# Three moves in a written-out order: the last low part of wo, the counting of tile 0, and the values' sums of the first pair

## The chip, the cores and the metric

The kernel runs on one core of a Trainium2 chip. The metric is the device time of one execution in microseconds; three runs of the kernel before took 380.36, 379.77 and 380.67, the median 380.36. Five engines work side by side, each in its own order: TensorE (PE, with its weight loads PEld), VectorE (DVE), ScalarE (ACT), GpSimd (POOL), and SyncE (SP), which issues transfers. An instruction that needs another engine's result waits for it, and everything behind it on its own engine waits too.

## The reference

x has 2048 rows of 512. Two branches are computed from it and mixed by a gate, `g*a + (1-g)*b` with `g = sigmoid(x . gate_w)`.

- Branch a is linear attention with 32 heads of 16: `q, k, v = x @ wqkv`; q and k go through a small matrix per head and two softmaxes over 16 (of the value and of its negative), which gives 32 features per head; `kv = phi_k^T v`, `z = sum phi_k`, `o = phi_q kv / (phi_q z)`, and `a = o @ wo`.
- Branch b is a choice of one of 256 experts per head: 32 heads, two scores over 16 keys each, the best key of each half; the pair names one of 256 rows of u and v; `b = sum over heads of gelu(x . u_e) * v_e`. The softmax is over one element, so it is 1. What is left is a count: how often each of the 256 experts was chosen by the 32 heads of a row, times gelu(x . u_e), times v.

## The kernel before

The rows are cut into 16 tiles of 128. Numbers are kept as a high and a low part (names ending in h and l): ScalarE casts the high part, VectorE or GpSimd subtracts it from the raw number, and three matmuls replace one. The order of every engine is the order in which the code is written (`manual_schedule`), so moving a line moves instructions on its engine.

**First half, up to about 125 us: keys, values and expert scores.** Tiles 0 to 4 are done one by one, tiles 5 to 14 in pairs (t, t+1) with t = 5, 7, 9, 11, 13. A pair shares matmuls by sums of its two tiles (class `Sums`). In a pair the banks a (pk), b (pu), c (pv), d (pk of the second tile) and e (pe) are built up with copies between them: `act.copy(b, a)` at line 487, `act.copy(c, b)` at 511, `act.copy(d, b)` at 543. The values of the second tile, vn, begin as a copy of e (line 554 in the first pair), and two sums follow on VectorE, vt = c + vn (557) and vn = b + vn (558). `k_exp` and `k_sum` (267, 271, 272) are the exponentials and sums of the key features. `Sums.high` (183) and `Sums.low` (189) make the high part gh and the low part gl of a tile's sum. The bank pu of the pair t = 7 is filled at line 487 once the pair before has read its bank by line 557.

**Second half: one turn of a loop for each tile a = 0 to 14**, with three tiles in flight: a (query projection, softmax differences and exponentials), b = a - 1 (comparison results counted, the query features transposed) and z = a - 2 (numerator, output). TensorE's order in a turn: `mid_num(z)` (matmuls oT from the transposed features pt and kvb, line 776), `front_q(a)` (pq, 56 to 58), `back(z)` (po: twelve matmuls at 888 with o's parts and wo's, then six at 895 with the coefficients ch and cl and the expert rows), `mid_mask(a)` (mk, 795), `front_s(a+1)` (the two halves of the scores s), `front_p(a+1)` (pp). The others feed it:

- `join(b)` (767), ScalarE: pt from two transposes tp; `mid_num` reads it in two halves.
- `count` (803 to 835), VectorE: a chain of 18 instructions, cut into steps by `yield`, that turns the mask into the counts cf. `step(b, n)` runs n steps, `drain(b)` the rest. Line 811 and 813 are one step. In turn 0 the first five steps of tile 0 have run; in turn 1 the rest runs.
- `coef` (839), GpSimd: cf times gelu (`gelu_out`, 662, is just ahead of it). `c_planes` (844, 846): ScalarE's copy plc and SyncE's transpose tpc. `c_join` (851, 855): ctj and the high part ch. `back_cl` (876): the low part cl on VectorE.
- `best(a+1, half)` (733, 734), VectorE: the maximum over 16 scores and the comparison with it; `turn_eq` (740) transposes the result (et).
- `soft_sum` (694), `soft_y` (704), VectorE: sums of tile a's exponentials and of the weighted w, which GpSimd makes at 690.
- `gelu_act` (656 to 658), ScalarE: the end of gelu for tile a.

The raw wo comes in late: two of its four pieces lie in rawo2, in the pool `late`. The last piece's high part is cast at line 984, its low part wol[3] is made at line 1041 (tile wbl, whose room it reuses). In turn 1 the pool `late` is closed and a new pool w4 is opened in its room; pt, plc, tpc, ctj, ch and cl lie in w4. The first join writes pt there, so it has to wait for the last reader of what lay there.

Of the kernel before, what the change touches and what calls it, by code (L numbers as in the profile page):

```python
# [16 lines left out]
ALU = mybir.AluOpType  # L17
# [18 lines left out]
def mix_kernel(ctx, tc, xT, wqT, wkT, wv, wphi, wo, wq, kk, ug, ev, cst, out):  # L36
    nc = tc.nc
    pe, dve, act, pool, sp = nc.tensor, nc.vector, nc.scalar, nc.gpsimd, nc.sync
# [210 lines left out]
    by16 = lambda a: a.rearrange("p (h f) -> p h f", f=F)  # L249
# [19 lines left out]
    def k_sum(t):  # L269
        d, st = phis[t], stk[t]  # L270
        dve.tensor_reduce(st[:, 64:128], g64(d), axis=AX.X, op=ALU.add)  # L271
        dve.reciprocal(st[:, 128:192], st[:, 64:128])
# [22 lines left out]
    def score_planes(j):  # L295
        pl = wa_.tile([P, 2, D], U16, tag="wpl", bufs=1, name=f"wpl{j}")
        act.copy(pl, wsP.pop(j).bitcast(U16).rearrange("p (c j) -> p j c", j=2))
        tp = wa_.tile([P, 8, P], U16, tag="wtp", bufs=1, name=f"wtp{j}")
        sp.dma_start_transpose(tp, pl.rearrange("p j c -> p (j c)"))
        joins.append((j, tp))  # L300
# [168 lines left out]
    for t in range(5, NT - 1, 2):  # L469
        n = t + 1  # L470
        more = [u for u in (t + 4, t + 5) if u < NT]
        for u in more:
            x_load(u)
        if t == NT - 5:
            rawu = [spare(ug[:, 0:2], "rawu0", [P, 2, NU])]
        elif t == NT - 3:
            rawu.append(spare(ug[:, 2:4], "rawu1", [P, 2, NU]))
            rawe = [spare(ev[:, 0], "rawe0", [P, D])]
        if behind:
            k_diffs(behind)  # L480
        for u in (t + 2, t + 3):
            if u < NT - 1 and u not in (7, 9):
                x_low(u)
        a = pks[t] = mm_bank(f"pk{t}")
        prod(a, tile_of(t, 0), b11, True)
        b = mm_bank(f"pu{t}")
        act.copy(b, a)
        if 5 < t < NT - 3:
            Sums.add(t + 2)
        if t == 5:  # L490
            (j1, tp), = joins
            joins.clear()
            tj1 = wa_.tile([P, D], F32, tag="wtj", bufs=1, name="wtj1")
            join_tp(j1, tp, tj1)
            score_planes(2)
            load_wq()
            load_wq()
            join_end(j1, tj1)
            Sums.add(t + 2)
        elif t < NT - 3:  # L500
            join_all()
        else:
            (j6, tp), = joins
            joins.clear()
            tj6 = wa_.tile([P, D], F32, tag="wtj", bufs=1, name="wtj6")
            join_tp(j6, tp, tj6)
        e = tr_bank(f"pe{t}")
        prod(e, sums(0, 2), b1, True)
        prod(b, sums(1, 0), b2, False)
        c = mm_bank(f"pv{t}")  # L510
        act.copy(c, b)
        if t == 5:
            k_exp(4)
            k_sum(4)
            k_mult(4)
            x_high(9)
            (j2, tp), = joins
            joins.clear()
            tj2 = wa_.tile([P, D], F32, tag="wtj", bufs=1, name="wtj2")
            join_tp(j2, tp, tj2)  # L520
        prod(a, tile_of(t, 2), b21, False)
        k_diffs(t)
        if behind:
            k_exp(behind)
            k_sum(behind)
            k_mult(behind)
        score(2, 5 < t < NT - 3)
        if t == NT - 3:
            rawq = stage(wqT, "rawq")
            score_planes(7)  # L530
        elif t > 5:
            load_wq()
            load_wq()
        for u in (t - 3, t - 2):
            kvacc(u)
        vn, vt = v_tile(n), v_tile(t)
        if t > 5:
            act.copy(vn, by16(e))
            k_exp(t)
            k_sum(t)  # L540
        prod(b, sums(0, 0), b3, False)
        d = pks[n] = mm_bank(f"pk{n}")
        act.copy(d, b)
        if t == 5:
            join_high(j2, tj2)
            score_planes(3)
            Sums.high(7, (0,))
            k_exp(t)
            x_low(9)
            k_sum(t)  # L550
        prod(c, sums(1, 2), b22, False)
        if t == 5:
            Sums.high(7, (1,))
            act.copy(vn, by16(e))
        if t == NT - 3:
            x_split(NT - 1)
        dve.tensor_tensor(vt, by16(c), vn, op=ALU.add)
        dve.tensor_tensor(vn, by16(b), vn, op=ALU.add)
        o2 = d.rearrange("p (c n) -> p c n", c=2)
        prod(o2, tile_of(n, 2), b4, False)  # L560
        if t + 3 < NT:
            if t > 5:
                Sums.high(t + 2)
            Sums.low(t + 2)
            if t == 5:
                join_low(j2, tj2)
        if t == 7:
            for i in range(2):
                x_parts(i, 11)
        for u in more if n < NT - 4 else ():  # L570
            if u != 9:
                x_high(u)
        k_mult(t)
        behind = n
    t = NT - 1
# [36 lines left out]
    def step(t, n=1):  # L612
        for _ in range(n):
            if t in chains and next(chains[t], None) is None:
                del chains[t]
# [221 lines left out]
    def coef(t):  # L837
        e = st8[t]
        (pool if t < NT - 2 else dve).tensor_tensor(e["C"], e["C"], e["G"], op=ALU.mult)

    def c_planes(t):
        e = st8[t]
        pl = w4.tile([P, 2, NX], U16, tag="plc", bufs=1, name=f"plc{t}")
        act.copy(pl, e["C"].bitcast(U16).rearrange("p (c j) -> p j c", j=2))
        e["tc"] = w4.tile([P, 4, P], U16, tag="tpc", bufs=1, name=f"tpc{t}")
        sp.dma_start_transpose(e["tc"], pl.rearrange("p j c -> p (j c)"))
# [124 lines left out]
    for a in range(NT - 1):  # L971
        n, b, z = a + 1, a - 1, a - 2
        owed = min(18, 3 * max(0, a - DEFER))
        left = min(18, 3 * max(0, a - DEFER + 1))
        B, Z = b >= 0, z >= 0
        if Z:
            mid_num(z)
        if a == 2:
            c_planes(z)
            gelu_pre(a)  # L980
        if a == 1:
            front_q(a)
            v15 = vproj(NT - 1)
            act.copy(woh[3], rawo[3])
        if B:
            planes(b, 0)
            if Z:
                c_join(z)
            if a == 1:
                v15()  # L990
            planes(b, 1)
        if a > 1:
            front_q(a)
        if owed:
            back(z - 1, owed)
            store(z - 1)
        gelu_in(a)
        if Z:
            num_lo(z)
        if B:  # L1000
            if a == 1:
                for _ in gate(a):
                    pass
                soft_in(a)
                step(b, 6)
            else:
                soft_in(a, dealt(a, b, z))
                drain(b)
        else:
            for _ in gate(a):  # L1010
                pass
        if a != 1:
            gelu_act(a)
        if a > 0:
            soft_exp(a)
        if Z and not left:
            back(z)
            store(z)
        if not left and a > 1:
            mid_mask(a)  # L1020
        if a:
            front_s(n, 0)
        if left or a == 1:
            mid_mask(a)
            if 0 < left < 18:
                back(z, 18 - left)
        if a == 1:
            kvacc(NT - 1)
            kv_final()
            cl_.close()  # L1030
            w4 = ctx.enter_context(tc_pool("w4", "right"))
        front_s(n, 1)
        front_p(n, False)
        soft_w(a)
        if a == 1:
            best(n, 0)
        soft_sum(a, 0)
        soft_sum(a, 1)
        if a == 1:
            drain(b)  # L1040
            dve.tensor_tensor(wol[3], rawo[3], woh[3], op=ALU.subtract)
        if a == 0:
            pool.tensor_tensor(wol[2], rawo[2], woh[2], op=ALU.subtract)
            step(a, 5)
        if a != 1:
            best(n, 0)
        if a == 0:
            best(n, 1)
            turn_eq(n)
        soft_y(a, 0)  # L1050
        soft_y(a, 1)
        soft_p(a)
        if B:
            join(b)
            gelu_out(b)
            coef(b)
            if a == 1:
                gelu_act(a)
            else:
                c_planes(b)  # L1060
        if a == 0:
            soft_b(a, lambda t: None)
        else:
            soft_b(a)
            best(n, 1)
            turn_eq(n)
        if a != 1:
            gelu_pre(n)
# [123 lines left out]
```

## Time and profile before

| | us |
|---|---|
| median of three runs | 380.36 (379.77 to 380.67) |
| profiled execution, its own time | 380.58 |
| its span, first to last instruction | 378.8 |
| TensorE busy | 367.2 (97%) |
| VectorE busy | 333.3 (88%) |
| ScalarE busy | 256.5 (68%) |
| GpSimd busy | 204.9 (54%) |

A line of the timeline gives start, duration, engine, line of the kernel, operation, output and inputs, shape, how many instructions were merged, and in brackets how long the engine stood idle before it and what ended that. Durations of TensorE overlap, since its matmuls are pipelined; there the distance between starts is what counts. A view by stages gives for each stretch its length and then the busy time of TensorE, its weight loads, VectorE, ScalarE and GpSimd with the number of instructions, the granted clock of TensorE, the share of the transfer engines and GB/s. The chain that ended last lies on TensorE for 83% of the span.

### The profile page before, as it was taken

To read this page: it belongs to the slowest core of one execution; us is meant where nothing else is said; L and a number is where in the kernel's file an instruction comes from. 1 tells how busy PE (TensorE), PEld (TensorE's weight loads), DVE (VectorE), ACT (ScalarE), POOL (GpSimd) and SP (SyncE) were. 2 spreads that over 40 slices of the span, in tenths; PEclk is the share of its full clock that TensorE was granted. 3 is DMA by queue.
4 is the path that set the end of the run, shared out by engine and by line. 5 is a ranking of instruction groups with operands and counts; after the bars stand their busy time and mean duration, and the time that the engine had idled before them with its cause. 6 is when DMAs were issued, how large, how long until landed. Compare 5 with 4: busy or idle time off the path is not lost.

```text
span 378.8 us, 8837 instructions
## 1 busy us (share of the span) xinstructions
PE 367.2 (97%) x3443; PEld 288.5 (76%) x3443; DVE 333.3 (88%) x786; ACT 256.5 (68%) x459; POOL 204.9 (54%) x205
## 2 busy tenths in 40 slices
PE   8999998999999999499999999999999999999995
PEld 4766766777778888378878888888888888888775
DVE  4679999989697799869999999999999999999993
ACT  4576678676656565648768677695686686687741
POOL 1189988978758746316426335354454464364700
PEclk9999999999999999789999999999999999999999
DMA  7867995656881212132361441441633523523201
GB/s 269 322 242 245 275 318 159 198 152 267 302 171 61 86 30 55 27 71 73 82 99 42 112 96 47 83 99 30 123 44 83 126 54 73 126 52 74 69 32 55
DMA packets 72074, 46.67 MB, mean 123 GB/s; under 512 B 63584, under 2 KB 64480, under 8 KB 69728
## 3 DMA queue, kind: packets, MB, share of 16 engines
q1 hardware_dynamic: 71168, 45.24, 44.1%
q10 hardware_dynamic: 864, 0.87, 0.9%
q8 instruction: 27, 0.44, 0.5%
q14 instruction: 15, 0.12, 0.1%
HBM read 26.43 MB, written 4.19 MB: 81 GB/s over the span
## 4 chain that ended last, share of the span: by engine, by line
PE 83%; issue 5%; DVE 4%; POOL 3%; ACT 3%; DMA 1%; SPq 0%; POOLq 0%; ACTq 0%; DVEq 0%
PE po L888 11%; PE s L56 6%; PE s L57 6%; PE s L58 6%; PE po L895 5%; PE pq L56 4%; PE pk L459 4%; PE pu L459 4%; PE ws L292 4%; PE pq L58 4%; PE pq L57 4%; PE oT L776 3%; PE kvacc L283 2%; PE pp L57 2%; PE pp L58 2%
## 5 line engine op out<-in xcount | busy, mean ns | idle before, releaser
L690 POOL TENSOR_TENSOR w<-d,zb 128x512 f32<-128x512 f32 x32 | 40.9, 1300 | 79.9 <-ACT d L684 79.9
L56 PE MATMUL s<-sh,xh 128*128 128x512 f32 x128 | 50.8, 397 | 0.0
L57 PE MATMUL s<-sl,xh 128*128 128x512 f32 x128 | 49.9, 390 | 0.0
L58 PE MATMUL s<-sh,xl 128*128 128x512 f32 x128 | 49.8, 389 | 0.0
L725 POOL TENSOR_TENSOR d<-d,st 128x512 f32<-128x512 f32 x30 | 31.3, 1064 | 28.4 <-DVE st L719 26.8
L684 ACT ACTIVATE d<-d 128x512 f32<-128x512 f32 x32 | 20.0, 632 | 37.1 <-DVE d L119 29.0
L767 ACT COPY pt<-tp 128x1024 uint16<-128x1024 uint16 x28 | 36.3, 1365 | 6.0 <-issue 6.0
L276 POOL TENSOR_TENSOR d<-d,st 128x1024 f32<-128x1024 f32 x16 | 32.6, 2036 | 9.4 <-ACT d L267 7.5
L757 ACT COPY pl<-d 128x1024 uint16<-128x1024 uint16 x28 | 29.2, 1044 | 5.1 <-POOL d L725 5.0
L58 PEld LDWEIGHTS s<-sh,xl 128*128 128x128 f32 x128 | 24.0, 188 | 5.0
L56 PE MATMUL pq<-wah,xh 128*128 128x512 f32 x64 | 27.8, 434 | 0.0
L56 PEld LDWEIGHTS s<-sh,xh 128*128 128x128 f32 x128 | 24.0, 188 | 4.7
L57 PEld LDWEIGHTS s<-sl,xh 128*128 128x128 f32 x128 | 24.1, 188 | 4.6
L58 PE MATMUL pq<-wah,xl 128*128 128x512 f32 x64 | 26.0, 406 | 0.0
L57 PE MATMUL pq<-wal,xh 128*128 128x512 f32 x64 | 25.9, 405 | 0.0
L734 DVE TENSOR_TENSOR eq<-s,mx 128x512 bf16<-128x512 f32 x32 | 22.1, 691 | 1.1
L694 DVE TENSOR_REDUCE st<-d 128x32 f32<-128x512 f32 x32 | 21.5, 681 | 1.4
L156 DVE TENSOR_TENSOR xl<-xr,xh 128x512 fp32r<-128x512 f32 (+2 forms) x17 | 20.3, 1208 | 1.7 <-ACT xh L152 1.6
L733 DVE TENSOR_REDUCE mx<-s 128x32 f32<-128x512 f32 x32 | 21.8, 680 | 0.0
L271 DVE TENSOR_REDUCE st<-d 128x64 f32<-128x1024 f32 x16 | 19.4, 1214 | 2.6 <-ACT d L267 2.1
L704 DVE TENSOR_REDUCE st<-w 128x32 f32<-128x512 f32 x32 | 20.5, 676 | 0.6 <-POOL w L690 0.5
L267 ACT ACTIVATE d<-d 128x1024 f32<-128x1024 f32 x16 | 17.1, 1066 | 4.1 <-DVE d L121 4.1
(272 smaller groups left out, 1125.0 us busy)
## 6 DMA issues: line engine op xcount, KB each, us to landing
wq<-wq SPq DMA_DIRECT2D x16, 1024.0 KB, 6.0
xr<-xT SPq DMA_DIRECT2D x15, 256.0 KB, 5.3
y<-ot SPq DMA_DIRECT2D x15, 256.0 KB, 2.2
rawk<-wkT SPq DMA_DIRECT2D x1, 1024.0 KB, 6.5
rawq<-wqT SPq DMA_DIRECT2D x1, 1024.0 KB, 6.9
rawu<-ug SPq DMA_DIRECT2D x2, 258.0 KB, 5.4
rawv<-wv ACTq DMA_DIRECT2D x2, 256.0 KB, 4.6
rawv<-wv SPq DMA_DIRECT2D x2, 256.0 KB, 5.7
```

The costliest lines, as they stand in the source:

```text
L56: pe.matmul(o, ah, bh, start=(first and i == 0), stop=False)
L57: pe.matmul(o, ah, bl, start=False, stop=False)
L58: pe.matmul(o, al, bh, start=False, stop=(last and i == n - 1))
L276: pool.tensor_tensor(g64(d), g64(d), b64(st[:, 128:192]), op=ALU.mult)
L459: pe.matmul(o, x_, w_, start=(first and i + j == 0), stop=(i == 1 and j == 2), skip_group_check=True)
L690: pool.tensor_tensor(hs(e["w"], i), hs(e["ph"], i), hs(zb, i), op=ALU.mult)
L725: eng.tensor_tensor(g64(d)[:, gs_], g64(d)[:, gs_], r[:, gs_].unsqueeze(2).to_broadcast([P, 32, F]), op=ALU.mult)
L733: dve.tensor_reduce(mx, p3, axis=AX.X, op=ALU.max)
L734: dve.tensor_tensor(e["eq"][:, 512 * half:512 * half + 512].rearrange("p (h f) -> p h f", f=F), p3, mx.unsqueeze(2).to_broadcast([P, H, F] ...
L757: act.copy(pl, e["ph"][:, halves[i]].bitcast(U16).rearrange("p (c j) -> p j c", j=2))
L767: act.copy(p16[:, :, 4 * i:4 * i + 4, :], e["tp"][i].rearrange("p (j g) n -> p j g n", j=2))
L888: pe.matmul(po, a, b, start=(i == 0), stop=False)
```

## The change

Nothing is added or removed: each engine runs the same instructions, and some stand elsewhere. There are three moves.

First, the low part wol[3] goes from behind the end of tile 0's counting to directly behind tile 1's four softmax differences. Second, of the counting of tile 0 only three steps (four instructions) run ahead of tile 2's first comparison and tile 1's sums, where six ran before; and `c_planes(0)` moves from the start of turn 2 to the end of turn 1, as in all later turns, which puts plc ahead of tile 1's gelu and tpc's transpose ahead of tile 2's et on SyncE. Third, in the pair t = 5 the copy of e into vn goes ahead of the high part, and the two sums of v go ahead of the key sums.

```diff
@@ pair t = 5 @@
             score_planes(3)
+            act.copy(vn, by16(e))
             Sums.high(7, (0,))
             k_exp(t)
             x_low(9)
-            k_sum(t)
         prod(c, sums(1, 2), b22, False)
         if t == 5:
             Sums.high(7, (1,))
-            act.copy(vn, by16(e))
...
         dve.tensor_tensor(vt, by16(c), vn, op=ALU.add)
         dve.tensor_tensor(vn, by16(b), vn, op=ALU.add)
+        if t == 5:
+            k_sum(t)
@@ turns of the loop @@
         if a == 2:
-            c_planes(z)
             gelu_pre(a)
...
                 soft_in(a)
-                step(b, 6)
+                dve.tensor_tensor(wol[3], rawo[3], woh[3], op=ALU.subtract)
+                step(b, 3)
...
         if a == 1:
             drain(b)
-            dve.tensor_tensor(wol[3], rawo[3], woh[3], op=ALU.subtract)
...
             coef(b)
+            c_planes(b)
             if a == 1:
                 gelu_act(a)
-            else:
-                c_planes(b)
```

The rows of the built programs show where the instructions stand. Line numbers of the change differ by one or so from those of the kernel before; names carry the tile's number ahead of the underscore. On VectorE, in turn 1, from the last difference of tile 1 on (d21), before:

```order
L121 TENSOR_TENSOR d21_1935<-st21_1936,pq1_1896 128x32x16
L811 TENSOR_TENSOR m10_1941<-sa0_63 128x64
L813 TENSOR_TENSOR m20_1942<-sa0_63 128x32
L821 TENSOR_TENSOR X0_1945<-m10_1941,m20_1942 128x256
L824 TENSOR_SCALAR T0_1946<-X0_1945 128x256
L825 TENSOR_TENSOR X0_1945<-X0_1945,T0_1946 128x512
L826 TENSOR_SCALAR T0_1946<-X0_1945 128x256
L827 TENSOR_SCALAR X0_1945<-X0_1945 128x256
L733 TENSOR_REDUCE mx0_2_2046<-s0_2_1954 128x32
L734 TENSOR_TENSOR eq2_2045<-s0_2_1954,mx0_2_2046 128x512
L694 TENSOR_REDUCE st21_1936<-d21_1935 128x32 x2
L828 TENSOR_TENSOR X0_1945<-X0_1945,T0_1946 128x512
```

And the same place in the change, where wbl is the low part of wo's last piece and stood before behind cf0, six rows after the last one shown above:

```order
L121 TENSOR_TENSOR d21_1935<-st21_1936,pq1_1896 128x32x16
L1005 TENSOR_TENSOR wbl_78<-rawo2_1719,wbh_77 128x512
L812 TENSOR_TENSOR m10_1942<-sa0_63 128x64
L814 TENSOR_TENSOR m20_1943<-sa0_63 128x32
L822 TENSOR_TENSOR X0_1946<-m10_1942,m20_1943 128x256
L825 TENSOR_SCALAR T0_1947<-X0_1946 128x256
L734 TENSOR_REDUCE mx0_2_2044<-s0_2_1952 128x32
L735 TENSOR_TENSOR eq2_2043<-s0_2_1952,mx0_2_2044 128x512
L695 TENSOR_REDUCE st21_1936<-d21_1935 128x32 x2
L826 TENSOR_TENSOR X0_1946<-X0_1946,T0_1947 128x512
L827 TENSOR_SCALAR T0_1947<-X0_1946 128x256
L828 TENSOR_SCALAR X0_1946<-X0_1946 128x256
```

The low part moved up by seventeen instructions, and three instructions of the counting moved behind comparison and sums.

On ScalarE, from the second half of the join of tile 0 (pt0) to the high part of its coefficients (ch0), before:

```order
L767 COPY pt0_2062<-tp1_0_1931 128x2x512
L656 ACTIVATE gs1_1888<-gs1_1888 128x1
L657 ACTIVATE x21_1892<-x21_1892 128x256
L658 ACTIVATE x21_1892<-x21_1892,gs1_1888 128x256
L780 CAST xh0_65<-oT0_0_2087 128x256
L780 CAST xh0_65<-oT1_0_2088 128x256
L844 COPY plc0_2107<-cf0_2056 128x512
L630 ACTIVATE gs2_2111<-pp2_2029 128x1
```

And in the change, where the copy plc0, which reads GpSimd's product cf0, comes first:

```order
L768 COPY pt0_2062<-tp1_0_1931 128x2x512
L845 COPY plc0_2067<-cf0_2057 128x512
L657 ACTIVATE gs1_1888<-gs1_1888 128x1
L658 ACTIVATE x21_1892<-x21_1892 128x256
L659 ACTIVATE x21_1892<-x21_1892,gs1_1888 128x256
L781 CAST xh0_65<-oT0_0_2091 128x256
L781 CAST xh0_65<-oT1_0_2092 128x256
L631 ACTIVATE gs2_2111<-pp2_2027 128x1
```

plc0 moved up past tile 1's gelu (three instructions) and the two casts of xh that TensorE's po reads.

On ScalarE in the first pair, from the planes of the scores (wpl3) to the bank pu of the next pair (pu7), before:

```order
L297 COPY wpl3_727<-ws3_641 128x1024
L183 CAST gh_81<-xr8_397 128x512
L267 ACTIVATE d5_635<-d5_635 128x1024
L183 CAST xh15_67<-xr7_359 128x512
L554 COPY v6_714<-pe5_607 128x32x16
L152 CAST xh0_65<-xr10_579 128x512
L487 COPY pu7_775<-pk7_768 128x512
```

And in the change:

```order
L297 COPY wpl3_727<-ws3_641 128x1024
L547 COPY v6_714<-pe5_607 128x32x16
L183 CAST gh_81<-xr8_397 128x512
L267 ACTIVATE d5_635<-d5_635 128x1024
L183 CAST xh15_67<-xr7_359 128x512
L152 CAST xh0_65<-xr10_579 128x512
L487 COPY pu7_775<-pk7_768 128x512
```

The copy of the values v6 moved up past the two casts and the exponential; on VectorE its two sums moved up past the key sums of tile 5 in the same way.

## The prediction

> **What bounds the kernel now.** I read the busy slices of the page first, then the stages, the chain, and at the holes of TensorE the timeline of each engine. The stages give TensorE's busy time as the second number:
>
> ```profile
> 125.00:158.00 33.00, 28.07 (x300) 22.77 (x300) 29.73 (x69) 18.38 (x44) 18.46 (x17) 0.98 0.21 50
> 158.00:365.00 207.00, 207.00 (x1477) 169.05 (x1470) 192.18 (x554) 149.64 (x284) 95.17 (x99) 0.99 0.36 77
> ```
>
> From 158 to 365 us TensorE is never idle; VectorE has 15 us to spare there. So a microsecond that TensorE gains before 158 comes off the end, unless a later wait takes it back. Between 125 and 158 it stands idle 4.93 us, nearly all in one place, the start of tile 2. TensorE's rows there, then the same five points one tile later, where nothing waits:
>
> ```profile
> 156.24 0.45 PE L776 MATMUL oT<-pt,kvb 64*32 64x128 f32 x16 [4.10 <-ACT pt L767]
> 157.44 0.68 PE L776 MATMUL oT<-pt,kvb 64*32 64x128 f32 x16 [0.75 <-ACT gs L656]
> ...
> 163.34 0.57 PE L888 MATMUL po<-t1h,xh 128*128 128x512 f32 x1
> ...
> 167.84 0.47 PE L56 MATMUL s<-sh,xh 128*128 128x512 f32 x1
> ...
> 174.92 0.67 PE L776 MATMUL oT<-pt,kvb 64*32 64x128 f32 x32
> ...
> 178.38 0.39 PE L888 MATMUL po<-t1h,xh 128*128 128x512 f32 x1
> ...
> 181.10 0.39 PE L895 MATMUL po<-eh,ch 128*128 128x512 f32 x1
> ...
> 182.68 0.47 PE L56 MATMUL s<-sh,xh 128*128 128x512 f32 x1
> ```
>
> The idle begins at 156.24 - 4.10 = 152.14. One tile later oT to po takes 3.46 us, po to its last six matmuls (L895) 2.72, those to s 1.58: 7.76 together. Here, from 152.14 to s, it took 15.70. So 7.9 us are lost in this one place: 4.85 by the two waits, the rest because matmuls ran slowly after them. The windows give the reason in the granted clock (third number from the end):
>
> ```profile
> 154.00:156.00 2.00, 0.00 (x0) 0.00 (x0) 2.00 (x6) 1.14 (x1) 1.02 (x1) 1.00 0.00 0
> 158.00:160.00 2.00, 2.00 (x13) 1.56 (x6) 1.54 (x4) 1.94 (x7) 1.62 (x2) 0.50 0.00 0
> ```
>
> After the idle the clock is at half; from 157.44 to po 5.90 us pass instead of 3.46, so the halving costs 2.4 us. [...]
>
> What ended the idle is ScalarE's join pt. ScalarE itself, before it and after:
>
> ```profile
> 154.86 2.53 ACT L767 COPY pt<-tp 128x1024 uint16<-128x1024 uint16 x2 [6.00 <-issue]
> 157.26 0.19 ACT L656 ACTIVATE gs<-gs 128x1 f32<-128x1 f32 x1
> ...
> 158.42 0.65 ACT L780 CAST xh<-oT 128x256 fp32r<-128x256 f32 x2
> 158.95 0.63 ACT L844 COPY plc<-cf 128x512 uint16<-128x512 uint16 x1
> ...
> 162.62 0.76 ACT L851 COPY ctj<-tpc 128x512 uint16<-128x512 uint16 x1 [0.81 <-DMA tpc<-plc]
> 163.42 0.40 ACT L855 CAST ch<-ctj 128x256 fp32r<-128x256 f32 x1
> ```
>
> ScalarE was free from 148.86 and the view names no releaser. VectorE's rows do:
>
> ```profile
> 144.94 0.72 DVE L811 TENSOR_TENSOR m<-sa 128x64 uint16<-128x64 uint16 x1
> ...
> 147.03 1.38 DVE L826 TENSOR_SCALAR T<-X 128x256 uint32<-128x256 uint32 x1
> ...
> 149.63 0.68 DVE L733 TENSOR_REDUCE mx<-s 128x32 f32<-128x512 f32 x1
> ...
> 150.95 1.27 DVE L694 TENSOR_REDUCE st<-d 128x32 f32<-128x512 f32 x2
> 152.13 0.41 DVE L828 TENSOR_TENSOR X<-X,T 128x512 uint16<-128x512 uint16 x1
> ...
> 153.75 0.42 DVE L835 TENSOR_TENSOR cf<-X 128x256 f32<-128x256 uint8 x1
> 154.09 0.68 DVE L1041 TENSOR_TENSOR wbl<-rawo,wbh 128x512 fp32r<-128x512 f32 x1
> ...
> 164.25 0.21 DVE L811 TENSOR_TENSOR m<-sa 128x64 uint16<-128x64 uint16 x1
> ...
> 165.83 0.29 DVE L826 TENSOR_SCALAR T<-X 128x256 uint32<-128x256 uint32 x1
> ```
>
> L1041, the low part of wo's last piece, ends at 154.77 and the join starts 0.09 us later. It is the last reader of the raw wo, which lies in the pool whose room pt takes; it stands behind the whole counting of tile 0.
>
> **Part 1, the low part behind tile 1's differences.** L1041 goes to where L811 stood, 144.94. There GpSimd works:
>
> ```profile
> 144.84 0.74 POOL L652 TENSOR_TENSOR x<-x,px 128x256 f32<-128x256 f32 x1
> 146.99 2.57 POOL L690 TENSOR_TENSOR w<-d,zb 128x512 f32<-128x512 f32 x2 [1.40 <-ACT d L684]
> 149.52 0.78 POOL L662 TENSOR_TENSOR px<-x,px 128x256 f32<-128x256 f32 x1
> 154.35 1.02 POOL L839 TENSOR_TENSOR cf<-cf,px 128x256 f32<-128x256 f32 x1 [4.05 <-DVE cf L835]
> ```
>
> L811 took 0.72 us beside L652 and 0.21 one tile later with GpSimd idle: 0.51 of standing still. I charge that to the subtraction: 144.94 + 0.51 + 0.68 = 146.13. [...]
>
> ```profile
> 144.97 2.66 SPq L759 DMA_TRANSPOSE tp<-pl  x2
> ```
> ```profile
> tp<-pl SPq DMA_TRANSPOSE x28, 3.2
> tpc<-plc SPq DMA_TRANSPOSE x14, 2.3
> ```
>
> The second was issued at about 146.3 and lands 3.2 later, 149.5. The join's halves run from 148.86 and about 150.2 to 151.4, before TensorE is free at 152.14. Both waits and the half clock go. Price gained if nothing else were late: 15.70 - 7.76 = 7.9 us. That is the ceiling.
>
> **Part 2, comparison and sums ahead of the rest of the counting, and plc ahead of gelu and casts.** Behind the subtraction stand four counting instructions (L811 to L824, 1.1 us by the 144.94 to 147.03 stretch less the standing still and L825): done at 147.1. Then comparison and sums, 149.63 to 152.13, 2.5 us: 149.6. They read beside GpSimd's L690 without loss (0.68 each there), while L826 took 1.38 beside it, against 0.29 alone. The nine steps left take 154.17 - 152.13 = 2.04 for six, and 0.41 + 0.29 + 0.29 for the other three, 3.1 with gaps: 152.7, and half a microsecond if L662 holds one up: 153.2 against 154.17. So the gain for cf is only 1 us. GpSimd's product starts 0.18 later and takes 0.75, like L652 (its 1.02 lay beside L1041, now gone): 154.15. I take plc's start as 154.4, bounds 154.0 and 155.6.
>
> Now the new wait. ScalarE is strictly in order, and plc stands ahead of gelu and casts; all of them, and TensorE's po behind them, wait for GpSimd. Gelu's three run 157.26 to 158.42, 1.16. So the casts start at 154.4 + 0.63 + 1.16 = 156.2, the first half is there at 156.55. TensorE wants it at 152.14 + 3.46 = 155.6: idle 0.95. Next, ch: from the casts' start to ch's end it took 163.82 - 158.42 = 5.40, of which plc's 0.63 has moved ahead and the wait of 0.81 goes (tpc is issued at 155.0, ahead of the comparison's transpose now, and lands 2.3 later, 157.4, long before the join of it at about 159): 3.96, so ch at 160.15. TensorE wants it at 156.55 + 2.72 = 159.3: idle 0.85. Then s at 160.15 + 1.58 = 161.75, against 167.84: **6.1 us** of the ceiling of 7.9. By the bounds of plc (s follows it by 7.35): 161.35 to 162.95, so 6.5 to 4.9. The comparison's transpose stands behind tpc's on SyncE now, by one issue of about 1.3; the comparison's second half is done at 157.6, when SyncE has long been free.
>
> **Part 3, the first pair.** A copy of v goes ahead of three casts on ScalarE, the sums of v ahead of the key sums on VectorE.
>
> ```profile
> 58.03 0.63 ACT L183 CAST gh<-xr 128x512 fp32r<-128x512 f32 x1
> 58.74 1.58 POOL L189 TENSOR_TENSOR gl<-xr,gh 128x512 fp32r<-128x512 f32 x1
> ...
> 60.03 0.59 ACT L554 COPY v<-pe 128x512 f32<-128x512 f32 x1
> ...
> 62.10 0.57 ACT L487 COPY pu<-pk 128x512 f32<-128x512 f32 x1 [0.96 <-DVE v L557]
> 62.72 0.50 PE L459 MATMUL pu<-uh,xh 128*128 128x512 f32 x1 [1.15 <-ACT pu L487]
> ```
>
> pu's copy waited 0.96 us for v's first sum and TensorE 1.15 for the copy. With v at 58.03 that sum runs before 60; the copy follows its queue at 61.1, TensorE at 61.7: 1.0 gained. Against it, gh moves back by 0.5, and gl with it; gl feeds matmuls just ahead of pu. If gl takes its 1.58 again, TensorE stands 0.5 there. Bounds 0.5 and 1.05; I take 0.9, nearer the copy's row, since part of gl's 1.58 was itself a collision with VectorE. VectorE's key sums move back behind the two sums of v; only GpSimd's product waits for them, and for that kvacc of the next pair, so I cost them at nothing; if that cover is gone, they cost what they moved.
>
> **The sum.** 6.1 + 0.9 = 7.0 us. The profiled execution took 380.58 (span 378.8 and 1.8 around it): 373.6. The median is 0.22 lower: **373.4**.
>
> **Rivals.** (1) The port goes against VectorE: L824 would start at about 146.85 and GpSimd's L690 at 146.99. If L824 comes second it stands some 1.1 us, as L826 did, and L662 may be held behind the counting. Then plc is at 155.6, the gain 4.9 + 0.9: 374.6. The margin is 0.14 us; chance 0.15. (2) The clock halves all the same, because two idles of 0.9 close together count like one: plus the 2.4 us, 375.8. Against it, the 1.15 at 62.72 halved nothing (its matmul took 0.50, like the 0.47 of s); 0.07. (3) The change doesn't free the join: its wait is for something else that ends at 154.8, and only the first pair stays, 379.5. The 0.09 us between L1041 and the join speaks against; 0.03. (4) Slower: ScalarE's queue, blocked by plc. s comes 7.35 after plc's start; from a plc at 160.5 on, nothing is left. If each of the nine steps stood 1.09 us like L826, plc would be at 164.2 and s at 171.55, 3.7 later than now: 383.2 with the first pair's 0.9. GpSimd has only L662's 0.78 to do meanwhile, so 0.02.
>
> **How the numbers follow.** My forecast has 0.73. The range goes from 372.2 (half of the two new idles gone, and all of the first pair) to 375.7 (rival 1 with no gain in the first pair is 375.5). A measurement here can tell about 0.2%, 0.76 us. Faster holds the forecast, rivals 1 and 2 and most of 3: 0.94; same 0.03; slower 0.03.
>
> **What would show it.** Right: no idle of TensorE of over 1.5 us between 140 and 170, the clock 1.00 there, pt about 3 us before TensorE is free, then two idles just under 1 us, ended by xh and by ch; pu 1 us earlier in the first pair. Wrong: half clock, pt late, or ch over 2 us late; or TensorE idle anew from tile 3 on, because VectorE, which gains less here than TensorE, can't follow.

## The result, and the profile after

The change takes 373.8 us (median of four runs, 373.46 to 374.25) against 380.51 for the kernel before on the same chip (379.77 to 380.88): a ratio of 0.9827, 95% interval 0.9808 to 0.9845. The profiled execution took 373.71 with a span of 371.9, so 6.87 less than the profiled one before, and 6.7 by the medians; 373.4 was forecast. Line numbers below are those of the kernel shown, one or so off those of the kernel before.

TensorE's rows at the places that were shown of before:

```profile
61.88 0.50 PE L459 MATMUL pu<-uh,xh 128*128 128x512 f32 x1
...
151.27 0.67 PE L777 MATMUL oT<-pt,kvb 64*32 64x128 f32 x32
...
155.50 0.50 PE L889 MATMUL po<-t1h,xh 128*128 128x512 f32 x1 [0.61 <-ACT xh L781]
...
159.12 0.50 PE L896 MATMUL po<-eh,ch 128*128 128x512 f32 x1 [0.60 <-ACT ch L856]
...
160.90 0.48 PE L56 MATMUL s<-sh,xh 128*128 128x512 f32 x1
```

oT has no bracket any more: it follows the matmul before it. Two brackets of 0.6 are left, ended by xh and by ch. From oT to s it takes 9.63 us, where it took 15.70 from the start of the idle: 6.07 less. The span from s to the end is the same to 0.1 (211.0 now; 378.8 - 167.84 = 211.0 before), so nothing is given back later. The rest, 0.87, had been gained when oT was reached: 152.14 without the wait before, 151.27 now. Of it pu's row shows 0.84.

The stages of TensorE, with its busy time as the second number and the granted clock third from the end:

```profile
125.00:158.00 33.00, 32.34 (x259) 26.21 (x259) 29.76 (x74) 22.21 (x54) 19.60 (x18) 1.00 0.25 55
...
158.00:365.00 207.00, 206.40 (x1518) 168.33 (x1517) 195.98 (x568) 149.12 (x283) 92.76 (x96) 1.00 0.38 78
```

The idle of 4.93 in the first stage is down to 0.66, the 0.60 of the second is the wait for ch, and the clock is 1.00 in both. So none of what would have shown the prediction wrong is there: no half clock, no late pt, no new idle from tile 3 on. VectorE (the fourth number) has 11 us to spare in the second stage, where it had 15.

What feeds oT, po and the six matmuls of L896 on ScalarE:

```profile
148.05 2.59 ACT L768 COPY pt<-tp 128x1024 uint16<-128x1024 uint16 x2
153.38 0.62 ACT L845 COPY plc<-cf 128x512 uint16<-128x512 uint16 x1 [2.74 <-POOL cf L840]
153.91 0.20 ACT L657 ACTIVATE gs<-gs 128x1 f32<-128x1 f32 x1
...
155.07 0.65 ACT L781 CAST xh<-oT 128x256 fp32r<-128x256 f32 x2
...
158.66 0.40 ACT L856 CAST ch<-ctj 128x256 fp32r<-128x256 f32 x1
```

The join starts at 148.05, 3.2 us before TensorE is free, and is done at 150.64, 0.6 before; the prediction's sign "about 3 us before" fits its start, not its end. ScalarE then stands for 2.74 us in front of plc, with gelu and the casts queued behind it. VectorE and GpSimd in the same stretch:

```profile
144.09 1.19 DVE L1005 TENSOR_TENSOR wbl<-rawo,wbh 128x512 fp32r<-128x512 f32 x1
...
146.00 0.29 DVE L825 TENSOR_SCALAR T<-X 128x256 uint32<-128x256 uint32 x1
146.21 0.68 DVE L734 TENSOR_REDUCE mx<-s 128x32 f32<-128x512 f32 x1
...
148.72 0.96 DVE L826 TENSOR_TENSOR X<-X,T 128x512 uint16<-128x512 uint16 x1
149.72 0.29 DVE L827 TENSOR_SCALAR T<-X 128x256 uint32<-128x256 uint32 x1
...
152.01 0.43 DVE L836 TENSOR_TENSOR cf<-X 128x256 f32<-128x256 uint8 x1
```
```profile
144.00 0.74 POOL L653 TENSOR_TENSOR x<-x,px 128x256 f32<-128x256 f32 x1
146.13 2.56 POOL L691 TENSOR_TENSOR w<-d,zb 128x512 f32<-128x512 f32 x2 [1.40 <-ACT d L685]
148.66 0.74 POOL L663 TENSOR_TENSOR px<-x,px 128x256 f32<-128x256 f32 x1
152.61 0.74 POOL L840 TENSOR_TENSOR cf<-cf,px 128x256 f32<-128x256 f32 x1 [3.20 <-DVE cf L836]
```

The low part took 1.19 beside L653, 0.51 more than the 0.68 of the kernel before (the row at 154.09). L825 began 0.13 us before GpSimd's product and took its 0.29; L826 began 0.06 after L663 and took 0.96.

### The profile page after: what moved, and what is told of

Read it like the earlier page. It is cut to its first block, busy times and chain, and to the rows that moved or that the text cites. A ratio compares the mean times of both kernels' runs of the same rounds, so it can differ in the third digit from the quotient of the medians.

```text
span 371.9 us, 8839 instructions
## 1 busy us (share of the span) xinstructions
PE 365.0 (98%) x3443; PEld 286.2 (77%) x3443; DVE 332.6 (89%) x786; ACT 256.3 (69%) x459; POOL 203.1 (55%) x205
## 4 chain that ended last, share of the span: by engine, by line
PE 83%; DVE 5%; POOL 3%; ACT 3%; issue 3%; DMA 2%; SPq 0%; POOLq 0%; ACTq 0%; DVEq 0%
PE po L889 10%; PE s L56 7%; PE s L57 6%; PE s L58 6%; PE po L896 6%; PE pk L459 5%; PE pu L459 4%; PE ws L292 4%; PE pq L56 4%; PE pq L58 3%; PE pq L57 3%; PE oT L777 2%; PE pe L459 2%; PE kvacc L283 2%; PE pv L459 2%
## 5 line engine op out<-in xcount | busy, mean ns | idle before, releaser
L691 POOL TENSOR_TENSOR w<-d,zb 128x512 f32<-128x512 f32 x32 | 40.9, 1297 | 76.8 <-ACT d L685 76.8
L56 PE MATMUL pq<-wah,xh 128*128 128x512 f32 x64 | 26.8, 418 | 0.0
L58 PE MATMUL pq<-wah,xl 128*128 128x512 f32 x64 | 25.1, 392 | 0.0
L57 PE MATMUL pq<-wal,xh 128*128 128x512 f32 x64 | 25.0, 390 | 0.0
L156 DVE TENSOR_TENSOR xl<-xr,xh 128x512 fp32r<-128x512 f32 (+2 forms) x17 | 21.7, 1288 | 1.7 <-ACT xh L152 1.6
```

What stands on the lines that cost most here:

```text
L56: pe.matmul(o, ah, bh, start=(first and i == 0), stop=False)
L57: pe.matmul(o, ah, bl, start=False, stop=False)
L58: pe.matmul(o, al, bh, start=False, stop=(last and i == n - 1))
L691: pool.tensor_tensor(hs(e["w"], i), hs(e["ph"], i), hs(zb, i), op=ALU.mult)
```

## The experiments

Twelve kernels in three groups; within a group all ran on one chip, beside the kernel before (380.08, 380.21 and 379.98). The change itself ran again in the third group only; where a kernel of the first two groups is compared with the change, the change's 373.8 comes from another chip. Nothing of the computation is left out in any of them.

| kernel | median us | ratio to before | interval |
|---|---|---|---|
| third move alone | 379.42 | 0.9978 | 0.9964 to 0.9991 |
| all but the third move | 374.67 | 0.9855 | 0.9834 to 0.9877 |
| low part moved alone | 380.98 | 1.0014 | 0.9998 to 1.0030 |
| change, plc and tpc back | 378.75 | 0.9957 | 0.9941 to 0.9972 |
| change, low part back | 378.14 | 0.9945 | 0.9926 to 0.9964 |
| change, six steps ahead | 376.52 | 0.9904 | 0.9882 to 0.9926 |
| change, five steps | 375.19 | 0.9874 | 0.9858 to 0.9891 |
| change, four steps | 374.14 | 0.9844 | 0.9830 to 0.9857 |
| change again | 373.71 | 0.9837 | 0.9816 to 0.9857 |
| gelu ahead of plc | 373.49 | 0.9816 | 0.9799 to 0.9834 |
| and the output ahead | 373.58 | 0.9819 | 0.9799 to 0.9839 |
| and cl earlier | 373.13 | 0.9818 | 0.9804 to 0.9831 |

**Do the two places add up?** The third move alone, on the kernel before:

```diff
             score_planes(3)
+            act.copy(vn, by16(e))
             Sums.high(7, (0,))
             k_exp(t)
             x_low(9)
-            k_sum(t)
...
         dve.tensor_tensor(vn, by16(b), vn, op=ALU.add)
+        if t == 5:
+            k_sum(t)
```

> The kernel before with the third move alone (copy of the values' bank ahead of the casts, sums of the values ahead of the key sums, in the pair t = 5). Theory: TensorE's 1.15 us of idle ahead of pu goes and comes off the end in full, since no later wait takes it back: 379.5 to 379.6 against 380.5, TensorE's idle at the start of tile 2 stays 4.1 and 0.75. Rival: the gain is eaten by the same idle at tile 2 (its join waits for VectorE, which was not moved by TensorE's microsecond): idle there grows to about 5, and the time stays at 380.5.

And the change without it:

> The changed kernel without the third move. Theory: the start of tile 2 alone is worth 6.1 us, so 374.4 to 374.8 against 380.5 before and 373.8 for the change; the two gains add up. Rival: the first pair matters only once the start of tile 2 is mended, or the other way round (the two don't add): 373.8, with TensorE idle 1.15 ahead of pu and nothing idle ahead of po or ch.

The first gives 379.42, 0.66 under its own before; by the ratio's interval 0.3 to 1.4. TensorE's idle at tile 2 is 4.08 and 0.51 there, not 5: the microsecond is not eaten. The second, 374.67, is 5.4 under its before and 0.87 above the change, and the bracket of 1.15 stands ahead of pu again:

```profile
62.52 0.50 PE L459 MATMUL pu<-uh,xh 128*128 128x512 f32 x1 [1.15 <-ACT pu L487]
```

Both theories held: the two places add. 0.66 and 5.41 make 6.07, against 6.71 for the whole change and 6.27 where it ran again (379.98 less 373.71); these medians can't tell that apart.

**Is the freed join all?** The low part alone, on the kernel before:

```diff
                 soft_in(a)
+                dve.tensor_tensor(wol[3], rawo[3], woh[3], op=ALU.subtract)
                 step(b, 6)
...
             drain(b)
-            dve.tensor_tensor(wol[3], rawo[3], woh[3], op=ALU.subtract)
```

> The kernel before with the first move alone: wol[3] directly behind tile 1's differences, then six steps of the counting as before, plc at the start of turn 2 behind gelu and casts. Rival (freeing the join is all): pt comes at about 151, the 4.1 us of idle and the half clock go, and most of the 6.1 us is gained: 374.6. Theory (the other moves are needed): the join is freed, but counting now meets GpSimd's product and cf comes at about 155, tpc is issued behind the comparison's transpose and lands at about 163, ch at about 164; TensorE's idle only moves from oT to the six matmuls that read ch, 4 to 6 us in one piece, the clock halves again, and the time is 379 to 382.

380.98: nothing gained. The join is free, oT starts at 153.55 without a bracket, and the idle stands behind it, in two pieces. TensorE, then the queue of transposes:

```profile
161.04 0.74 PE L888 MATMUL po<-t1h,xl 128*128 128x512 f32 x2 [2.06 <-DVE xl L787]
...
165.63 0.79 PE L895 MATMUL po<-eh,ch 128*128 128x512 f32 x1 [3.03 <-ACT ch L855]
```
```profile
160.68 1.23 SPq L740 DMA_TRANSPOSE et<-eq  x1
162.02 1.21 SPq L846 DMA_TRANSPOSE tpc<-plc  x1
```

plc was ready at 158.10, and tpc still went at 162.02: SyncE waited first for the comparison. From oT to s 15.08 us pass, hardly less than 15.70, and this execution also has the collision that the last section tells of. The theory held in outline; that VectorE's low part xl would also be late, by 2.06, it did not say.

**What is plc's place worth?** The change with `c_planes(0)` back at the start of turn 2:

```diff
         if a == 2:
+            c_planes(z)
             gelu_pre(a)
...
-            c_planes(b)
             if a == 1:
                 gelu_act(a)
+            else:
+                c_planes(b)
```

> The changed kernel with plc and tpc back at the start of turn 2 (behind gelu and casts on ScalarE, behind the comparison's transpose on SyncE). Theory: ScalarE's casts come early enough and po starts without a wait, but tpc is queued behind the comparison's transpose and lands at about 160.2 instead of 156.4, ch at about 161.4; TensorE stands idle nearly 4 us ahead of the six matmuls that read ch, s is 2.1 later: 375.9, and 378.4 if an idle of that length halves the clock. Rival (the rival of the prediction in which plc's blocking of ScalarE is the cost): undoing it removes the 0.6 of idle ahead of po and costs nothing: 373.0 to 373.2.

378.75, 5.0 more than the change, by the theory's upper branch. TensorE and the queue:

```profile
161.37 0.80 PE L896 MATMUL po<-eh,ch 128*128 128x512 f32 x1 [3.40 <-ACT ch L856]
```
```profile
156.42 1.23 SPq L741 DMA_TRANSPOSE et<-eq  x1
157.76 1.21 SPq L847 DMA_TRANSPOSE tpc<-plc  x1
```

In the change tpc goes first:

```profile
154.03 1.19 SPq L847 DMA_TRANSPOSE tpc<-plc  x1
156.57 1.23 SPq L741 DMA_TRANSPOSE et<-eq  x1
```

So plc's block of ScalarE is the small side of this move; its other side, tpc ahead of et on SyncE, is what keeps the gain.

**Is the low part's move needed once the counting is reordered?** The change with wol[3] back behind `drain(b)`:

```diff
                 soft_in(a)
-                dve.tensor_tensor(wol[3], rawo[3], woh[3], op=ALU.subtract)
                 step(b, 3)
...
             drain(b)
+            dve.tensor_tensor(wol[3], rawo[3], woh[3], op=ALU.subtract)
```

> The changed kernel with wol[3] back behind the end of tile 0's counting; the moves of the counting, of plc and of the first pair are kept. Theory: the join waits for wol[3] again, now at about 153 instead of 154.8; oT starts at about 154.4 after 3.2 us of idle, s about 2.1 later than in the change: 375.9; by the run in which 3.4 us of idle halved the clock, and 2.06 followed by 0.5 of work did too, the clock halves here as well and it is 378.6. Rival (the first move is not needed once the counting is reordered): the join is not late, 373.8.

378.14, near the 378.6 of the case in which the clock halves, and it did (below). VectorE, ScalarE and TensorE:

```profile
153.87 0.68 DVE L1041 TENSOR_TENSOR wbl<-rawo,wbh 128x512 fp32r<-128x512 f32 x1
```
```profile
154.63 2.53 ACT L768 COPY pt<-tp 128x1024 uint16<-128x1024 uint16 x2 [4.84 <-issue]
```
```profile
156.02 0.45 PE L777 MATMUL oT<-pt,kvb 64*32 64x128 f32 x16 [2.92 <-ACT pt L768]
157.22 0.68 PE L777 MATMUL oT<-pt,kvb 64*32 64x128 f32 x16 [0.74 <-ACT pt L768]
```

The low part ends at 154.55 and the join starts 0.08 later; in the kernel before it was 0.09. With the low part at either place the join goes with it: that this is the wait is now shown, not only read from two times that lie close.

**What do steps beside GpSimd's product cost, and when does the clock halve?** Four, five and six steps in place of three:

```diff
-                step(b, 3)
+                step(b, 4)
```

> The changed kernel with four steps of the counting instead of three ahead of the comparison. Theory (each step beside GpSimd's product stands 1.0 to 1.1 us): L826 takes 1.4 there instead of 0.96 behind the sums, all else alike; cf 0.4 to 0.5 later, the idle ahead of po 1.05 instead of 0.6, no halved clock: 374.2 to 374.4. Rival (what makes six steps dear is only the length of the halved clock): 373.8.

> The same with five steps. Theory: L826 and L827 stand, cf 1.4 later than in the change, the idle ahead of po about 2.0. Six steps gave 2.4 us of idle, a clock halved for 3.3 us, and 376.5. If an idle of about 2.0 halves the clock too, 375.8 to 376.3; if it takes more than that, 375.1 to 375.3.

> The changed kernel with six steps of the counting, as before, ahead of tile 2's comparison instead of three. Theory (what stands beside GpSimd's product stands still): the two or three more counting instructions stand about 1.1 us each, the cf is some 1.5 to 2 us later than 152.4, plc at 155 or later, the idle ahead of po grows from 0.6 to about 2.3: 375.4 to 375.9; up to 378 if an idle of that length halves the clock. Rival (the order of the counting doesn't matter, only the freed join and plc's place do): cf and plc stay within 0.3 us of the change, 373.8.

374.14, 375.19 and 376.52; the change itself on the chip of the first two:

> The changed kernel once more, as the base for the three others on the same chip: 373.8, with TensorE's two idles of 0.6.

It gave 373.71. VectorE with six steps:

```profile
147.61 1.40 DVE L826 TENSOR_TENSOR X<-X,T 128x512 uint16<-128x512 uint16 x1
149.04 1.27 DVE L827 TENSOR_SCALAR T<-X 128x256 uint32<-128x256 uint32 x1
150.35 0.72 DVE L828 TENSOR_SCALAR X<-X 128x256 uint32<-128x256 uint32 x1
```

Beside GpSimd they take 1.40, 1.27 and 0.72, in the change 0.96 (there the first of them begins 0.06 behind GpSimd's next product, L663), 0.29 and 0.29. Counted from the start of oT, cf ends 1.17 later in the change, and 1.58, 2.57 and 2.97 later with four, five and six steps. The idle ahead of po is 0.61, 1.02, 2.01 and 2.39. In the profiled execution with five steps the clock stayed at 1.00 throughout, in the one with six it fell to 0.50. TensorE's po with five steps, then with six, then the windows with six, the granted clock third from the end:

```profile
156.45 0.50 PE L889 MATMUL po<-t1h,xh 128*128 128x512 f32 x1 [2.01 <-ACT xh L781]
```
```profile
158.59 0.50 PE L889 MATMUL po<-t1h,xh 128*128 128x512 f32 x1 [2.39 <-ACT xh L781]
```
```profile
158.80:159.20 0.40, 0.40 (x3) 0.32 (x3) 0.36 (x2) 0.37 (x4) 0.40 (x1) 1.00 0.13 21
159.20:159.60 0.40, 0.40 (x3) 0.31 (x2) 0.40 (x2) 0.40 (x2) 0.40 (x2) 0.53 0.00 0
...
162.40:162.80 0.40, 0.40 (x3) 0.26 (x2) 0.36 (x3) 0.40 (x1) 0.00 (x0) 0.71 1.09 218
162.80:163.20 0.40, 0.40 (x3) 0.35 (x2) 0.40 (x3) 0.40 (x3) 0.00 (x0) 1.00 1.09 209
```

The four-step kernel is 0.4 above the change, five steps 1.5, six 2.7. All three theories held, four steps 0.06 under its range. The code alone does not settle whether the clock halves. Of the four executions with five steps, one had a mean granted clock of 0.994, the same as the profiled one with six steps, and took 376.22, as forecast for a halved clock; the other three, at 1.00, took 374.61 to 375.22. Of the six with six steps one stayed at 1.00 and took 375.85, as forecast for a clock that stays whole.

**Can the two idles of 0.6 be had too?** First gelu ahead of plc, and tile 0's cl ahead of four steps:

```diff
             coef(b)
-            c_planes(b)
             if a == 1:
                 gelu_act(a)
+            c_planes(b)
...
+            if a == 2:
+                back_cl(z)
             step(b, 4)
-            if z >= 0:
+            if z >= 0 and a != 2:
                 back_cl(z)
```

> The changed kernel with tile 1's gelu ahead of plc at the end of turn 1 (in ScalarE's 2.74 us of idle), and, in tile 2's turn, the low part cl ahead of four counting instructions on VectorE. Theory (plc's blocking of ScalarE is what the two idles of 0.6 are made of): xh comes 1.16 earlier, both idles go or fall under 0.25, s at about 160.0 instead of 160.9; then oT of tile 3 finds pt's second half at 167.65 and gives 0.3 back: 373.0 to 373.2 against 373.8. Rival (the next limit takes it all: VectorE's low part xl and cl, or the join of tile 1): 373.7.

Then, besides, tile 0's output ahead of tile 2's exponentials:

```diff
+        if a == 2:
+            back(z)
+            store(z)
         if a > 0:
             soft_exp(a)
-        if Z and not left:
+        if Z and not left and a != 2:
             back(z)
             store(z)
```

> The same with, besides, tile 0's output copied ahead of tile 2's exponentials on ScalarE (into its idle of 1.73 us), so that the join of tile 1 runs half a microsecond earlier. Theory: pt is no longer late for tile 3, all of the 0.9 is kept: 372.9. Rival: the same as without it, 373.1 or 373.7.

Then cl behind one step in tile 2's turn and behind two in tile 3's:

```diff
+            early = {2: 1, 3: 2}.get(a, 4)
-            step(b, 4)
+            step(b, early)
             if z >= 0:
                 back_cl(z)
+            step(b, 4 - early)
```

> The kernel with gelu ahead of plc and tile 0's output ahead of the exponentials, with the low part cl two or three counting instructions earlier on VectorE in the turns of tiles 2 and 3. Theory (VectorE, without idle from 153 to 177, is the next bound; there TensorE waits 0.3 for cl of tile 1): the idle goes, 0.4 more is kept, 373.1 to 373.2 against 373.8 for the change and 373.5 without this edit. Rival (VectorE has to do all of it anyway, so the wait comes back one turn later): 373.5.

373.49, 373.58 and 373.13, where the theories had 373.0 to 373.2, 372.9 and 373.1. Against 373.8 and 373.71 for the change the first two moved less than half as far as expected, too little for these medians to tell. In the first, s comes 8.94 after oT instead of 9.63, and TensorE gives part of it back in the next turn:

```profile
168.00 0.45 PE L777 MATMUL oT<-pt,kvb 64*32 64x128 f32 x16 [0.25 <-ACT pt L768]
```

In the second, pt is in time, but cl comes at 173.89 where its matmul would start at 174.06, and it starts at 174.36. VectorE and TensorE:

```profile
173.89 0.42 DVE L877 TENSOR_TENSOR cl<-ctj,ch 128x256 fp32r<-128x256 f32 x1
```
```profile
174.36 0.73 PE L896 MATMUL po<-eh,cl 128*128 128x512 f32 x2
```

So my theory fell for these two, and the rival (the next limit takes it) held for most of the gain. With cl earlier as well, from oT of tile 2 to the cl matmul of tile 3 it takes 23.15 us, where the change run again takes 23.81: 0.66 kept. The medians of that group differ by 0.58; their intervals overlap, so that it is faster than the change rests on the trace more than on the times.

## Why the prediction was right, step by step

- **Ceiling and the start of tile 2.** 6.1 was forecast; the trace gives 6.07 between oT and s, and the kernel with all but the third move 5.4 by the medians of its group. The forecast lateness of po and ch was 0.95 and 0.85; it was 0.77 (155.50 against 151.27 + 3.46) and 0.90 (159.12 against 155.50 + 2.72). From ch to s another 0.20 was not foreseen. A small part of it is cl, ready at 160.06: with gelu ahead of plc cl is there in time, and ch to s takes 1.71, where it takes 1.78 in the change and 1.58 one tile later without any wait. The rest appears behind the idle: the first matmul after it is followed by the next in 0.33 instead of 0.23. Together 1.87 against 1.80; that the sums agree so well is in part luck, since 0.18 too much at po and these 0.20 cancel. The profiled execution took 373.71 where 373.6 was forecast. The other 0.3 between 373.8 and 373.4 comes from taking the median 0.22 below the profiled execution, as in the kernel before; in the change it lies 0.09 above.
- **Part 1.** The low part took 0.68 + 0.51, as charged: GpSimd's L653 had begun 0.09 before it. The join was free of it. That the join needs it was worth 0.97 of my chances; the kernel with the low part back shows it.
- **Part 2.** The comparison took its 0.68 beside GpSimd's L691 (146.21 and 146.13), as forecast. plc was forecast to start 2.26 after the free start of oT and started 2.11 after it; the end of cf was forecast 1.06 after it and came 1.17 after it. From the casts' start to ch's end 3.96 was forecast and 3.99 measured. What I priced as the cost of plc's new place was right (0.77 at po), but I named its gain only in passing, as a wait of 0.81 that goes. Undone, it costs 5.0: tpc then stands behind et on SyncE, and goes 3.9 us after plc is ready (153.85 to 157.76).
- **Part 3.** 0.9 was forecast. pu starts 0.84 earlier although this execution ran 0.2 later up to there (pv's first matmul 56.13 against 55.93), so the place gives 1.04; gl costs 0.13 of delay within pe. The times say 0.66 and 0.87.
- **The rivals.** Rival 1, in which a counting step comes second to GpSimd's product (the rows show starts and durations; a port, as the prediction calls it, no run shows): L825 came first by 0.13 us, as forecast (0.14). But the price was mis-sized: I gave 1.2 us to one step that comes second. The nearest test is the four-step kernel, where another step, L826, comes second; it is 0.4 later, since the step that stands there (1.39) need no longer stand behind the sums (0.96). Rival 2: the clock stayed whole with two idles of 0.6; two of 0.9 did not occur. The price of the halved clock was read too low: 2.4 sets 5.90, counted from the second half of oT, against 3.46, counted from its first. The prediction's own 7.9 less the two waits of 4.85 gives about 3.1. Rival 4: ScalarE's block cost 0.77 at po: plc came 2.11 after oT, where the slower rival begins at 8.4 (160.5 - 152.14).
- **Undoing any one of the parts costs more than its share.** Low part back 4.3, plc back 5.0, counting back 2.7: 12.0 for a gain of 6.1 in this place. In the profiled executions each of the three brings an idle of over 2.3 us in one piece (2.92, 3.40 and 2.39), and the clock falls to 0.50 with it.

## What to carry to other kernels

Here the idle of the bounding engine was not made by one wait alone: behind the join stood SyncE's order and VectorE's counting, and freeing the first alone gained nothing. Before a wait is removed, find the next two in line, in every queue, the one of the transfers included, and move all of them or none. With six steps, 2.39 us of idle ahead of po in the profiled execution, the clock fell in that one and, by the mean granted clock (0.994 or 0.995), in five of the six; where that is so, the last part of such a repair is worth the most, since it is the one that brings the clock back.

## What the runs showed of the hardware

**The clock was at half for 3.41 us or twice that, and the shortest idle in or behind which it fell was 2.06 us.** From windows of 0.4 or 0.2 us at both ends, half clock ran from 159.22 to 162.63 with six steps (the windows above: 0.53 means 0.94 of 0.40 at half), from 156.90 to 160.32 with the low part back, and twice as long in the others: 160.68 to 167.51 with plc back, 161.69 to 168.52 with the low part alone, 156.88 to 163.70 in the kernel before. Two rows for that last one, the granted clock third from the end:

```profile
156.80:157.00 0.20, 0.00 (x0) 0.00 (x0) 0.20 (x2) 0.20 (x1) 0.00 (x0) 0.69 0.00 0
163.60:163.80 0.20, 0.20 (x2) 0.12 (x2) 0.20 (x1) 0.20 (x2) 0.00 (x0) 0.75 1.10 210
```

The lengths are 3.41, 3.42, 6.83, 6.83 and 6.82. The clock fell behind idles of 2.06 (low part alone), 2.39 (six steps), 2.92 (low part back, with part of a second one of 0.74) and 4.10 (the kernel before, with part of a second one of 0.75), and within one of 3.40 (plc back). In the 3.41 us before the clock fell TensorE had been busy for 40% (1.35 us, low part alone), 30% (six steps) and less; in the kernel before, from 150.06 to 153.47, it was busy for 61%, and the clock stayed at 1.00 until 156.88. Behind a single idle of 2.01 it did not fall in the profiled execution with five steps, though by the mean granted clock (0.994) it fell in another of the four executions of the same code. What sets these cases apart is not shown: only one execution of each kernel has a trace. Where the stretch of half clock lay also changed what the halving cost: with the third move alone the same 4.1 us of idle (4.08) came with a half clock from 154.26, before oT had started, and from the start of the idle to s it took 1.06 us less than before, 0.24 of that by a shorter second wait.

**A collision: the same subtraction took 0.69 us or 2.38.** At 109.5 us, far from the change, VectorE's low part of x meets GpSimd's product of the keys. In the change VectorE starts 0.02 ahead; VectorE, then GpSimd:

```profile
109.63 0.69 DVE L156 TENSOR_TENSOR xl<-xr,xh 128x512 fp32r<-128x512 f32 x1 [0.23 <-ACT xh L152]
```
```profile
109.65 2.47 POOL L276 TENSOR_TENSOR d<-d,st 128x1024 f32<-128x1024 f32 x1
```

With six steps, where this place has the same code, GpSimd is first by 0.10:

```profile
109.50 2.38 DVE L156 TENSOR_TENSOR xl<-xr,xh 128x512 fp32r<-128x512 f32 x1 [0.24 <-ACT xh L152]
```
```profile
109.40 1.94 POOL L276 TENSOR_TENSOR d<-d,st 128x1024 f32<-128x1024 f32 x1
```
```profile
111.94 0.50 PE L58 MATMUL pk<-wah,xl 128*128 128x512 f32 x1 [1.14 <-DVE xl L156]
```

VectorE takes 1.69 longer (2.38 against 0.69), and TensorE stands for 1.14. Four of the profiled executions have this wait of TensorE (1.14 with six steps, 1.16 with the low part back, 1.2 with the low part alone and in the last kernel); the others don't. In the kernel before GpSimd's recorded start is 0.01 ahead (110.46 against 110.47) and VectorE still takes its 0.69, so at that distance the recorded starts don't tell who came first. What decides who has to stand is not shown. The collision is a likely part of the spread within one kernel, 1.2 to 2.3 us in eight of the twelve, beside the halved clock; that is not shown, and putting xl where GpSimd is idle was not tried.
